# Block-sparse attention and an MLP: neighbouring values reloaded once a batch, neighbouring keys multiplied where they lie

## The chip, the cores and the metric

The kernel runs on one core of a Trainium2 chip. The metric is the device time of one execution in microseconds. A core has TensorE (PE in the profile, with its weight loads listed apart as PEld), VectorE (DVE), ScalarE (ACT), GpSimd (POOL) and SyncE (SP, which here issues DMAs only). Each engine takes its own queue in order, and semaphores hold it where its data is not ready.

## The reference

Block-sparse attention over q, k, v of (4 batches, 8 heads, 768 positions, 64), then an MLP over the 3072 tokens of 512 values:

```python
scores = np.matmul(q, k.transpose(0, 1, 3, 2)) / np.sqrt(D)
mask = np.abs(blk_i - blk_j) <= 1                      # blocks of 32, 24 of them
mask |= (blk_i == 0) | (blk_j == 0) | (blk_i == 23) | (blk_j == 23)
for qb in range(24):
    for kb in sampled_blocks[qb]:                      # 3 random blocks
        mask[qb*32:(qb+1)*32, kb*32:(kb+1)*32] = True
attn = softmax(np.where(mask, scores, -1e9))
x = np.matmul(attn, v).transpose(0, 2, 1, 3).reshape(3072, 512)
h = x @ w_in                                           # 512 x 2048
g = np.maximum(h, 0) ** 2
out = g @ w_out                                        # 2048 x 512
```

Inputs and output are float32; `sampled_blocks` (24, 3) is read at run time.

## The kernel before

All arithmetic on the chip has bf16 operands and float32 sums. Two heads share the 128 partitions, so there are 16 units u (batch u // 4, head pair u % 4). The stages are:

**Batches 0 and 1: dense.** Scores of 256 queries (places q0 = 0, 256, 512) against all keys (`scores`), `exps` on ACT, a product with 0/1 masks on DVE (`masks`), `values` with a column of ones for the sum, `normalize` on DVE (L387: a reciprocal at L391 and a product at L393 into a tile `xq` of one unit). In batch 1 each unit's `xq` is then transposed into the tile xT by a DMA that SP issues (`x_transp_dma`, L415); xT holds the four units of a place, and the MLP tile of that place waits for all four.

**Batches 2 and 3: sparse, in six visits v.** A visit takes two groups g = 2v and 2v+1 of 64 queries. Group 0 holds the first and last block, which see all keys (6 chunks of 128). Every other group sees 3 chunks: chunk 0 is the neighbouring four blocks, chunks 1 and 2 hold the two edge blocks and six sampled ones.
- Keys: `k_gather` (L548, on POOL or DVE) loads the sampled block numbers into registers (`blocks_of`, L531), then copies from the transposed keys QKT into the tile KG: chunk 0 (L558), the edge blocks where they are not there yet (L561, L562) and six sampled ones (L564).
- Values: `v_store` (L509) writes the batch's values VB to DRAM as rows. For each visit `v_gather` (L538) fetches the sampled rows into the tile VG (an indirect DMA on POOL, L543, or block by block from SP with register offsets, L546), and `v_window` (L516) the edge rows (L524) and the neighbouring rows (L528).
- `s_scores` (L566) multiplies, `s_exps` (L585, ACT), `s_masks` (L591, DVE), `s_values` (L597), `s_normalize` (L621, DVE, tile `xs`) and `s_transp` (L629, a DMA transpose into xT).

**The table** of the visits (`table_slots`, L452 on) is worked out once from the sampled blocks: row numbers for the indirect DMAs and the masks MKS.

**The MLP** runs in tiles of 256 tokens: `hidden` (four 128-wide slices of d_ff into one PSUM tile), `relu` (ACT L671 or DVE L673), `square`, `output`, `out_copy`, `store`. `w_load` brings the weights through POOL's queue.

Matrix products whose contraction fits use `pair` (L186): the same product on the two halves of 64 rows of the array, one after the other (form 64*128 in the profile). The sparse `s_values` at L618 uses 128 rows and 64 columns (128*64), the first batch's `values_full` and a few others 128*128.

The order of all work is written out: each step is a Task, and `PROGRAM` (L932) is a string of words, each an engine letter, a task number and, behind a slash, a PSUM spot. `run_program` goes through it and hands each instruction to its engine's queue in that order; `Buf` counts who holds a rotating buffer. So an engine is never rescheduled: an instruction that waits holds up all behind it on its engine. The raw inputs pass through `cast_qk` (float32 to bf16, L118 in the profile for all `copy` on POOL or DVE) and `transp_dma`.

The functions that are touched follow, with the profile's line numbers.

Of the kernel before, what the change touches and what calls it, by code (L numbers as in the profile page):

```python
# [19 lines left out]
P = 128  # L20
# [5 lines left out]
def kernel(  # L26
# [65 lines left out]
    def run_program(bufs):  # L92
# [3 lines left out]
        for word in PROGRAM.split():  # L96
            i, _, spot = word[1:].partition("/")
            t = tasks[int(i)]
            assert not t.done and all(d.done for d in t.deps)
            for b in t.get:  # L100
                if b.pool == "X":
                    b.at = int(spot)
                    old, cells[b.at] = cells[b.at], b
                else:
                    taken[b.pool].append(b)
# [21 lines left out]
    raw = {}  # L127

    def load(u, w, e):
        b, a = divmod(u, HP)  # L130
        name = ("qs", "ks", "vs")[w]
        t = ld.tile([P, 2, NCH, D], F32, name=name, tag=name, bufs=NRAW - (w > 0))
# [9 lines left out]
    KGT = [consts.tile([P, HP, 2, 3 * P], BF, name=f"KG{i}") for i in range(KG_BUFS)]  # L142

    def load_part(eng, u, w, ns):
        if u not in raw:
            raw[u] = [ld.tile([P, 2, NCH, D], F32, name=n, tag=n, bufs=NRAW - (n != "qs")) for n in ("qs", "ks", "vs")[:3 if u < 2 else 1 if u == 2 else 0]]
            if u == 2:
                raw[u] += [KGT[0].rearrange("p a i c -> p (a i c)").bitcast(F32)[:, 0:2 * NCH * D]]
            elif u == 3:
                raw[u] += [KGT[i].rearrange("p a i c -> p (a i c)").bitcast(F32)[:, j:j + 2 * NCH * D] for i, j in ((0, 2 * NCH * D), (1, 0))]  # L150
            if u >= 2:
                raw[u].append(work.tile([P, 2 * d_model], F32, name="ys", tag="ys", bufs=YS_BUFS))
# [25 lines left out]
    place = work.tile([P, TWM], F32, name="r", tag="r", bufs=R_BUFS).bitcast(BF)[:, 0:S]  # L178
# [39 lines left out]
    pre = work.tile([P, TWM], F32, name="r", tag="r", bufs=R_BUFS)[0:nb]  # L218
# [29 lines left out]
    MK, vg_at, vg_of = {}, {}, {}  # L248
    VGT = [consts.tile([P, 6 * H * VR], BF, name=f"VG{i}") for i in range(VG_BUFS)]

    def mk_claim(c0, e):
        MK[c0] = VGT[len(vg_at) % VG_BUFS][:, 0:NCH * QW].rearrange("p (n c) -> p n c", n=NCH)
        vg_at[c0] = len(vg_at) % VG_BUFS
# [19 lines left out]
    def cast_qk(u, w, ns, e):  # L273
        c = work.tile([P, NCH, 2, D], BF, name="qc", tag="qc", bufs=QC_BUFS)[:, ns]
# [68 lines left out]
    def exps(a, e):  # L343
        n = a[2] * len(a[3])
        pT = work.tile([P, 2, 512], BF, name="pT", tag="pT", bufs=PT_BUFS)
# [40 lines left out]

    def normalize(u, q0, w, e):  # L387
# [4 lines left out]
        xq = work.tile([P, 2, 2, D], BF, name="xq", tag="xq", bufs=XQ_BUFS)[:, 0:n]  # L392
        V.tensor_tensor(out=xq.rearrange("p c h d -> p h c d"), in0=po[:, :, :, 0:D], in1=rs.broadcast_to([P, 2, n, D]), op=AOP.mult)  # L393
        xtile[u, q0] = xq
# [11 lines left out]
    def x_tile(b, c0):  # L406
        if (b, c0) not in xT:
            xT[b, c0] = work.tile([P, HP, QW], BF, name="xT", tag="xT", bufs=XT_BUFS)
# [22 lines left out]
    dup, low = consts.tile([GR, SL - 4], F32, name="dup"), {}  # L431
    HB = block // 2
# [11 lines left out]
    def table_places(e):  # L444
        G.iota(ids[:, 0:4], pattern=[[1, 4]], base=0, channel_multiplier=2, **small)
# [6 lines left out]
    def table_slots(e):  # L452
        tmp = work.tile([P, TWM], F32, name="r", tag="r", bufs=R_BUFS)
# [4 lines left out]
        low[0] = work.tile([P, TWM], F32, name="r", tag="r", bufs=R_BUFS)[0:D].bitcast(BF)[:, 0:5 * P].rearrange("g (s c) -> g s c", c=P)  # L458
# [4 lines left out]
        for s_ in range(n):  # L463
            V.tensor_reduce(out=dup[:, s_:s_ + 1], in_=eq[:, s_, 0:4 + s_], axis=AX.X, op=AOP.max)
# [11 lines left out]
        def spread(j, of):  # L476
            to = low[0][0:GR, j].rearrange("g (k i) -> g k i", i=HB)
            V.tensor_copy(out=to[:, 0:RS], in_=of[:, 6:SL, None].broadcast_to([GR, RS, HB]))
            V.tensor_copy(out=to[:, RS:n], in_=of[:, 4:6, None].broadcast_to([GR, 2, HB]))

        for a in range(2):
            V.tensor_copy(out=low[0][0:GR, a].rearrange("g (e k i) -> g e k i", e=2, i=HB), in_=al[:, None, a, 0:4, None].broadcast_to([GR, 2, 4, HB]))
            spread(2 + a, al[:, a])
        spread(4, ids)
# [27 lines left out]
    def v_claim(b, v, e):  # L512
        vg_at[b, v] = len(vg_at) % VG_BUFS
        vgt[b, v] = VGT[vg_at[b, v]].rearrange("p (s c) -> p s c", s=6)
# [23 lines left out]
    def v_gather(b, v, i, e):  # L538
# [3 lines left out]
        if e == "POOL":  # L542
            G.indirect_dma_start(out=to[0:RS * HB], out_offset=None, in_=pairs, in_offset=bass.IndirectOffsetOnAxis(ap=idx[0:RS * HB, g - 1:g], axis=0))  # L543
        else:
            for j, r in enumerate(blocks_of(g, mybir.EngineType.SP)):
                sy.dma_start(out=to[j * HB:(j + 1) * HB], in_=pairs[bass.ds(r * HB, HB)])  # L546

    def k_gather(b, v, g, e):  # L548
# [7 lines left out]
        to = KGT[n][:, :, g % 2].bitcast(I32).rearrange("p a (z e j) -> p a z e j", z=3, e=2)  # L556
        rows = to[:, :, 1:3].rearrange("p a z e j -> p a z (e j)")
        eng.tensor_copy(out=to[:, :, 0], in_=src[:, :, :, 2 * w * (g - 1):2 * w * (g + 1)])  # L558
        if there.get((n, g % 2)) != b:
            there[n, g % 2] = b  # L560
            eng.tensor_copy(out=rows[:, :, :, RS * w:(RS + 1) * w], in_=src[:, :, :, 0:w])  # L561
            eng.tensor_copy(out=rows[:, :, :, (RS + 1) * w:], in_=src[:, :, :, (nb - 1) * w:nb * w])  # L562
        for r_ in range(RS):
            eng.tensor_copy(out=rows[:, :, :, r_ * w:(r_ + 1) * w], in_=src[:, :, :, bass.ds(at[r_] * w, w)])  # L564

    def s_scores(u, v, gs, buf, e):  # L566
        b, a = divmod(u, HP)
        i, ps, at = u % NPB, tile_of(buf), 0
        for g in gs:
            for c in range(chunks_of(g)):  # L570
                def keys(rows):
                    if g == 0:
                        return QK[i][rows, 1].rearrange("r (e p m) -> r e m p", e=2, m=CP)[:, c % 2, c // 2]
                    return KGT[kgt[b, v]][rows, a, g % 2, c * P:(c + 1) * P]
# [6 lines left out]
                pair(lambda h: ps[:, h, at:at + D], lambda h, rows: keys(rows), lambda h, rows: queries(rows), start=at == 0, stop=True)  # L581
# [3 lines left out]
    def s_exps(u, v, gs, e):  # L585
        n = sum(D * chunks_of(g) for g in gs)
        pT = work.tile([P, 2, 512], BF, name="pT", tag="pT", bufs=PT_BUFS)
# [33 lines left out]
    def s_normalize(b, v, e):  # L621
# [3 lines left out]
        xs = work.tile([P, HP, 2, D], BF, name="xs", tag="xs", bufs=2)  # L625
# [35 lines left out]
    def relu(T, f, e):  # L661
# [3 lines left out]
        r = work.tile([P, TWM], F32, name="r", tag="r", bufs=R_BUFS)[:, 0:n * w]  # L665
# [9 lines left out]
        gunit[T, f] = work.tile([P, TWM], BF, name="g", tag="g", bufs=G_BUFS)  # L675
# [45 lines left out]
    def out_copy(T, i, y, e):  # L721
        w = y[1] * (y[2][1] - y[2][0])
        ys = work.tile([P, 2 * d_model], F32, name="ys", tag="ys", bufs=YS_BUFS)[:, 0:w]
# [29 lines left out]

    def prepare(u):
# [4 lines left out]
        if u >= HP:  # L759
            g = gate[GATES[min(u - HP, len(GATES) - 1)]]  # L760
            old = [u - HP if u < HP + n_ else u - n_ for n_ in (NRAW, NRAW - 1, NRAW - 1)]
            ld_t = [T_(load, u, w, deps=cq[old[w], w] + [g]) for w in range(3)]
            at = [ld_t[2]]
            for w in (1, 0):
                qc = Buf("qc")
                c = T_(cast_qk, u, w, ALL, get=[qc], deps=[ld_t[w]])
# [3 lines left out]
        else:  # L770
            at = []
            for w, ns in [(1, ns) for ns in (KEYS if u == 0 else (ALL,))] + [(0, ns) for ns in QRS]:
                qc, hb = Buf("qc"), Buf("X")
                c = T_(cast_qk, u, w, ns, get=[qc])
# [4 lines left out]
        cv[u] = [T_(cast_v, u, deps=at + old_v)]  # L779
# [6 lines left out]

    def x_get(b, c0):
        if (b, c0) in xb:
            return {}
        xb[b, c0] = Buf("xT")  # L790
        return dict(get=[xb[b, c0]])

    def attend(a, add):
        u, q0, w, cs = a
        xb_, st, pt = Buf("X"), Buf("S"), Buf("pT")
        deps = [ev[u][1, n] for n in cs] + [ev[u][0, n] for n in range(q0 // P, (q0 + w) // P)]
# [222 lines left out]
```

## Time and profile before

| | us |
|---|---|
| runs | 266.87, 271.15, 262.80 |
| median of the 3 | 266.87 |
| the profiled execution | 263.07 |
| its span, first to last instruction | 261.3 |
| PE busy, 20 to 100 us of the span (first dense batches, MLP begins) | 79.05 of 80 |
| PE busy, 100 to 220 us (sparse batches, MLP) | 111.46 of 120 |
| PE busy, 220 to 261.3 us (last sparse visits, MLP) | 37.25 of 41.3 |

The mean granted clock of TensorE is 0.993. The costliest groups of the page, as far as the change touches them:

| line, operation | count | busy us | mean ns |
|---|---|---|---|
| L188 matmul of scores from KG, 64*128, 64 columns | 528 | 16.1 | 192 |
| L543 indirect DMA of sampled rows (POOL) | 21 | 20.1 | 958 |
| L564 copy of a sampled key block (POOL) | 114 | 25.0 | 265 |
| L558 copy of the neighbouring keys (POOL) | 19 | 8.1 | 428 |
| L118 cast of q (POOL) | 19 | 10.3 | 567 |
| L118 cast of k (POOL) | 13 | 8.8 | 699 |

How to read it: the span lies inside the time, which has 1.8 us around it. A matmul's own duration (192 ns) is from its start to the end of its flow through the array; matmuls overlap, so the pace is read from starts. "Busy" is the union of such times. What a line in square brackets or behind an arrow names is the event that ended an engine's idle time. Profile times are one execution's, while the runs differ by 3% among themselves.

### The profile page before, as it was taken

How to read it: one execution, taken by the hardware profiler on the slowest of the kernel's cores; microseconds unless marked ns; L12 is line 12 of the kernel's file. 1: busy time of each engine (PE TensorE's matmuls, PEld its weight loads, DVE VectorE, ACT ScalarE, POOL GpSimd, SP SyncE). 2: the span in 40 equal slices, each digit the busy share in tenths (PEclk: the TensorE clock that was granted, in tenths of full speed). 3: DMA queues.
4: the chain of work that ended last, by engine and by line, in shares of the span. 5: the costliest groups of instructions: out<-in, count | busy, mean ns of one | idle time of the engine just before them, and what ended most of it. 6: DMA issues, size and time to landing. Idle time of an engine off the chain costs nothing.

```text
span 261.3 us, 12047 instructions
## 1 busy us (share of the span) xinstructions
PE 244.1 (93%) x5265; PEld 186.4 (71%) x5265; DVE 155.5 (60%) x332; ACT 185.4 (71%) x218; POOL 118.1 (45%) x260
## 2 busy tenths in 40 slices
PE   6898999999999999986799989899999997999993
PEld 4766888679776599854676869757767775767683
DVE  7588879798989888574085634757646433520000
ACT  1799999999999899856397527855765857234640
POOL 2355571112046102496076797486475871143220
PEclk9999999999999999999799999999999999999999
DMA  6999999999879959959997999995953755112022
GB/s 183 373 266 176 251 180 272 215 239 238 222 243 205 220 136 208 171 130 231 228 241 160 204 203 224 245 236 107 264 118 116 160 95 151 23 23 80 3 99 67
DMA packets 64627, 47.08 MB, mean 180 GB/s; under 512 B 31599, under 2 KB 60656, under 8 KB 64576
## 3 DMA queue, kind: packets, MB, share of 16 engines
q1 hardware_dynamic: 58464, 37.48, 63.6%
q0 software_dynamic: 5568, 8.45, 18.3%
q8 instruction: 41, 0.67, 1.1%
q10 hardware_dynamic: 544, 0.39, 0.5%
q14 instruction: 10, 0.08, 0.1%
HBM read 35.51 MB, written 7.91 MB: 166 GB/s over the span
## 4 chain that ended last, share of the span: by engine, by line
PE 81%; DVE 6%; DMA 5%; ACT 4%; issue 2%; SPq 1%; DVEq 1%; POOL 0%; ACTq 0%; POOLq 0%
PE X L188 74%; PE X L618 4%; ACT pT L346 3%; DMA xT<-xq 2%; DMA xT<-xs 2%; PE X L384 2%; DVE pT L595 2%; DVE r L673 1%; SPq L417 1%; DVE QKT L118 1%; ACT pT L588 1%; DVE xq L393 0%; DVEq L533 0%; PE X L291 0%; DVE KG L564 0%
## 5 line engine op out<-in xcount | busy, mean ns | idle before, releaser
L188 PE MATMUL X<-xT,w_in_sb 64*128 64x256 bf16 x1536 | 101.9, 271 | 5.8 <-DMA xT<-xq 4.0
L188 PE MATMUL X<-w_out_sb,g 64*128 64x512 bf16 (+3 forms) x960 | 97.3, 334 | 1.4 <-issue 1.3
L188 PEld LDWEIGHTS <-w_in_sb 64*128 64x128 bf16 x1536 | 77.2, 95 | 18.0 <-issue 5.3
L346 ACT ACTIVATE pT<-X 128x1024 bf16<-128x1024 f32 x72 | 70.6, 1031 | 7.7 <-PE X L188 7.0
L588 ACT ACTIVATE pT<-X 128x768 bf16<-128x768 f32 (+1 forms) x56 | 41.5, 762 | 36.1 <-PE X L188 36.1
L188 PEld LDWEIGHTS <-g 64*128 64x128 bf16 x960 | 42.3, 94 | 25.2 <-issue 1.6
L684 POOL TENSOR_TENSOR g<-r 128x512 bf16<-128x512 f32 (+1 forms) x20 | 27.3, 1374 | 45.4 <-ACT r L671 27.2
L595 DVE TENSOR_TENSOR pT<-pT,MKS 128x768 bf16<-128x768 bf16 (+1 forms) x48 | 29.0, 637 | 23.1 <-ACT pT L588 23.1
L353 DVE TENSOR_TENSOR pT<-pT,VG 128x1024 bf16<-128x1024 bf16 x60 | 40.4, 708 | 2.1 <-ACT pT L346 1.9
L682 ACT ACTIVATE g<-r 128x1024 bf16<-128x1024 f32 (+1 forms) x40 | 37.2, 944 | 3.4 <-DVE r L673 3.2
L671 ACT ACTIVATE r<-X 128x1024 f32<-128x1024 f32 x27 | 28.5, 1064 | 14.0 <-PE X L188 13.6
L188 PE MATMUL X<-QKT 64*128 64x256 bf16 (+1 forms) x384 | 31.9, 254 | 1.0 <-DVE QKT L118 0.7
L673 DVE TENSOR_SCALAR r<-X 128x1024 f32<-128x1024 f32 x21 | 25.6, 1222 | 11.7 <-PE X L188 7.1
L564 POOL COPY KG<-QKT 128x64 int32 x114 | 25.0, 265 | 0.0
L543 POOL DMA_INDIRECT VG<-rows,idx x21 | 20.1, 958 | 10.2 <-DMA rows<-VB 3.7
L188 PEld LDWEIGHTS <-QKT 64*128 64x128 bf16 x384 | 16.5, 97 | 5.8 <-issue 1.0
L118 POOL CAST qc<-qs 128x384 bf16<-128x384 f32 (+3 forms) x19 | 10.3, 567 | 20.3 <-DMA qs<-in_q_dram 17.5
L188 PEld LDWEIGHTS <-KG 64*128 64x128 bf16 x528 | 14.6, 96 | 6.0 <-POOL KG L564 1.3
L118 POOL CAST qc<-ks 128x384 bf16<-128x384 f32 (+1 forms) x13 | 8.8, 699 | 21.3 <-DMA ks<-in_k_dram 18.9
L188 PEld LDWEIGHTS <-pT 64*128 64x128 bf16 x768 | 15.8, 94 | 3.1
L188 PE MATMUL X<-QKT,KG 64*128 64x64 bf16 x528 | 16.1, 192 | 1.5 <-POOL KG L564 0.8
L188 PE MATMUL X<-VB,pT 64*128 64x65 bf16 x768 | 17.4, 190 | 0.0
(101 smaller groups left out, 195.1 us busy)
## 6 DMA issues: line engine op xcount, KB each, us to landing
vs<-in_v_dram SPq DMA_DIRECT2D x14, 384.0 KB, 3.9
ks<-in_k_dram SPq DMA_DIRECT2D x13, 384.0 KB, 4.9
qs<-in_q_dram SPq DMA_DIRECT2D x12, 384.0 KB, 5.3
out_dram<-ys SPq DMA_DIRECT2D x9, 512.0 KB
VG<-rows SPq DMA_DIRECT2D x20, 132.0 KB, 6.6
w_in_sb<-in_moe_w_in_dram POOLq DMA_DIRECT2D x4, 512.0 KB, 9.0
w_out_sb<-in_moe_w_out_dram POOLq DMA_DIRECT2D x4, 512.0 KB, 7.6
rows<-VB SPq DMA_DIRECT2D x2, 792.0 KB
```

The source lines that it names most:

```text
L118: (V if e == "DVE" else G).tensor_copy(out=out, in_=in_)
L188: last = nc.tensor.matmul(out(r ^ crossed), lhsT(r ^ crossed, rows), rhs(r ^ crossed, rows), skip_group_check=True, **kw)
L346: A.activation(out=pT[:, :, 0:n], in_=stile.pop(a)[:, :, 0:n], func=AF.Exp, scale=scale)
L353: V.tensor_tensor(out=pT, in0=pT, in1=m[:, None].broadcast_to([P, 2, len(cs), w]), op=AOP.mult)
L543: G.indirect_dma_start(out=to[0:RS * HB], out_offset=None, in_=pairs, in_offset=bass.IndirectOffsetOnAxis(ap=idx[0:RS * HB, g - 1:g], axis=0))
L564: eng.tensor_copy(out=rows[:, :, :, r_ * w:(r_ + 1) * w], in_=src[:, :, :, bass.ds(at[r_] * w, w)])
L588: A.activation(out=pT[:, :, 0:n], in_=stile.pop((u, v, gs))[:, :, 0:n], func=AF.Exp, scale=scale)
L595: V.tensor_tensor(out=pT, in0=pT, in1=m[:, None].broadcast_to([P, 2, n]), op=AOP.mult)
L671: A.activation(out=to, in_=src, func=AF.Relu)
L673: V.tensor_scalar(out=to, in0=src, scalar1=0.0, scalar2=None, op0=AOP.max)
L682: A.activation(out=g, in_=r, func=AF.Square)
L684: (G if e == "POOL" else V).tensor_mul(out=g, in0=r, in1=r)
```

## The change

Six things, all in one edit:

1. Rotating buffers (raw inputs, r, ys, pT, g, qc, xq, xT) become named tiles; a Buf learns in `run_program` which of them it has, in the order of the plan.
2. In batch 1 the normalized values of the four units of a place go into one tile XS, and one `x_transp_dma` per place issues two transposes of 512 columns in place of four units' transposes of 256: 12 DMAs become 6.
3. Values: VB becomes the first six columns of a tile W of 11. After `v_store`, three `v_window` tasks a batch (two DMAs each) reload all 11 neighbouring windows into it, for all visits; the per-visit windows and the edge rows' DMAs are gone (24 and 12 DMAs before, 12 in all after). Visit 0 waits for all three windows, later visits for theirs. The gathers of sampled rows fetch the edge rows too (128 rows for 96); VG shrinks from six slots to four.
4. Keys: chunk 0 is no longer copied into KG (22 copies of 128x256 int32 are gone). It is multiplied where it lies in QKT, even and odd positions apart, as two pairs of 64 rows by 64 columns, each into half of the output partitions. The six chunks of group 0 are done in the same way. 272 matmuls of the form 64*128 become 544 of the form 64*64.
5. The table: eight reductions become one masked product and one reduction, six spreading copies become three, with one more iota.
6. A new PROGRAM. Of the 22 k_gathers, 13 are on POOL and 9 on DVE (19 and 3 before). Of the 22 v_gathers, three are on SP (one before). Of the q and k casts of units 4 to 15, 9 are on POOL and 15 on DVE (17 and 7 before). Three output copies move from ACT to DVE, and three of the table's mask casts too; three x copies of batch 0 likewise.

```diff
+    KGT = [consts.tile([P, HP, 2, 2 * P], BF, name=f"KG{i}") for i in range(KG_BUFS)]
+    W = [consts.tile([P, GR, H, VR], BF, name=f"W{i}") for i in range(2)]
...
-        VB.append(consts.tile([P, NCH, H, VR], BF, name=f"VB{i}"))
+        VB.append(W[i][:, 0:NCH])
...
-        xq = work.tile([P, 2, 2, D], BF, name="xq", tag="xq", bufs=XQ_BUFS)[:, 0:n]
+        b, a = divmod(u, HP)
+        xq = XS[:, :, a] if b else XQ[buf_of["xq", u, q0].at][:, 0:n]
...
-    def x_transp_dma(u, q0, w, e):
-        b, a = divmod(u, HP)
-        sy.dma_start(out=x_tile(b, q0)[:, a].rearrange("r (c p) -> r c p", p=P),
-                     in_=xtile.pop((u, q0)).rearrange("p c h d -> p (c h d)"), transpose=True)
-        otile.pop((u, q0))
+    def x_transp_dma(b, q0, e):
+        for c in range(2):
+            sy.dma_start(out=x_tile(b, q0)[:, :, c * P:(c + 1) * P], in_=XS[:, c].rearrange("p a h d -> p (a h d)"), transpose=True)
...
-        for s_ in range(n):
-            V.tensor_reduce(out=dup[:, s_:s_ + 1], in_=eq[:, s_, 0:4 + s_], axis=AX.X, op=AOP.max)
+        V.scalar_tensor_tensor(out=eq, in0=before, scalar=0.0, in1=eq, op0=AOP.is_gt, op1=AOP.mult)
+        V.tensor_reduce(out=dup, in_=eq, axis=AX.X, op=AOP.max)
...
-    def v_window(b, v, e):
-        gs = [g for g in VISITS[v] if g]
-        i0 = 2 - len(gs)
+    def v_window(b, w0, w1, e):
         w = H * VR
-        if vg_of.get(vg_at[b, v]) != b:
-            vg_of[vg_at[b, v]] = b
-            for j, r in enumerate((0, nb - 1)):
-                rows = rows_of[b][block * r:block * r + 1]
-                sy.dma_start(out=vgt[b, v][(RS + j) * HB:(RS + j + 1) * HB, 0:4],
-                             in_=bass.AP(rows.tensor, rows.offset, [[2 * w, HB], [0, 2], [1, 2 * w]]))
-        rows = rows_of[b][D * (gs[0] - 1):D * (gs[0] - 1) + 1]
+        rows = rows_of[b][D * w0:D * w0 + 1]
         for e_ in range(2):
-            sy.dma_start(out=vgt[b, v][e_ * D:(e_ + 1) * D, 4 + i0:6],
-                         in_=bass.AP(rows.tensor, rows.offset + e_ * w, [[2 * w, D], [D * w, 2 - i0], [1, w]]))
+            sy.dma_start(out=W[b % 2][e_ * D:(e_ + 1) * D, w0:w1].rearrange("p n h c -> p n (h c)"),
+                         in_=bass.AP(rows.tensor, rows.offset + e_ * w, [[2 * w, D], [D * w, w1 - w0], [1, w]]))
...
-            for j, r in enumerate(blocks_of(g, mybir.EngineType.SP)):
-                sy.dma_start(out=to[j * HB:(j + 1) * HB], in_=pairs[bass.ds(r * HB, HB)])
+            for j, r in enumerate([0, nb - 1] + list(blocks_of(g, mybir.EngineType.SP))):
+                sy.dma_start(out=to[j * HB:(j + 1) * HB], in_=pairs[r * HB:(r + 1) * HB] if j < 2 else pairs[bass.ds(r * HB, HB)])
...
     def k_gather(b, v, g, e):
...
-        eng.tensor_copy(out=to[:, :, 0], in_=src[:, :, :, 2 * w * (g - 1):2 * w * (g + 1)])
...
     def s_scores(u, v, gs, buf, e):
...
-                def keys(rows):
-                    if g == 0:
-                        return QK[i][rows, 1].rearrange("r (e p m) -> r e m p", e=2, m=CP)[:, c % 2, c // 2]
-                    return KGT[kgt[b, v]][rows, a, g % 2, c * P:(c + 1) * P]
+                def keys(rows, e):
+                    return QK[i][rows, 1].rearrange("r (e j) -> r e j", e=2)[:, e, D * c:D * (c + 1)] if g == 0 else QK[i][rows, 1].rearrange("r (e j) -> r e j", e=2)[:, e, block * (g - 1):block * (g + 1)]
...
-                pair(lambda h: ps[:, h, at:at + D], lambda h, rows: keys(rows), lambda h, rows: queries(rows), start=at == 0, stop=True)
+                if g and c:
+                    pair(lambda h: ps[:, h, at:at + D], lambda h, rows: KGT[kgt[b, v]][rows, a, g % 2, (c - 1) * P:c * P], lambda h, rows: queries(rows),
+                         start=at == 0, stop=True)
+                else:
+                    for e_ in range(2):
+                        pair(lambda h: ps[e_ * D:(e_ + 1) * D, h, at:at + D], lambda h, rows: keys(rows, e_), lambda h, rows: queries(rows),
+                             start=at == 0, stop=True)
                 at += D
...
-                        if g == 0:
-                            val = VB[b % 2][:, c].rearrange("p h c -> p (h c)")[:, cols]
-                        elif c == 0:
-                            val = vgt[b, v][:, 4 + i, cols]
+                        if c == 0 or g == 0:
+                            val = W[b % 2].rearrange("p n h c -> p n (h c)")[:, g - 1 if g else 2 * c, cols]
...
-        parts.append(T_(v_window, b, v, deps=[vw, cl]))
+        parts += [wins[i] for i in ((0, 1, 2) if v == 0 else sorted({(g - 1) // 4 for g in VISITS[v]}))]
...
+            wins = [T_(v_window, b, w0, min(w0 + 4, GR), deps=[vw]) for w0 in range(0, GR, 4)]
```

More of the change, by code (lines that the diff above doesn't have):

```diff
@@ L177 @@
     V.memset(bm, 0.0)
-    place = work.tile([P, TWM], F32, name="r", tag="r", bufs=R_BUFS).bitcast(BF)[:, 0:S]
+    place = RT[0].bitcast(BF)[:, 0:S]
     blk = consts.tile([P, nb + 1], F32, name="blk")
@@ L217 @@
     edge = consts.tile([nb, 2], F32, name="edge")
-    pre = work.tile([P, TWM], F32, name="r", tag="r", bufs=R_BUFS)[0:nb]
+    pre = RT[1][0:nb]
     pm = pre[:, 0:2 * nb].rearrange("q (i j) -> q i j", i=2)
@@ L273, in cast_qk @@
     def cast_qk(u, w, ns, e):
-        c = work.tile([P, NCH, 2, D], BF, name="qc", tag="qc", bufs=QC_BUFS)[:, ns]
+        c = QC[buf_of["qc", u, w, ns.start].at][:, ns]
         if w < 2 and u >= SB * HP:
@@ L344, in exps @@
         n = a[2] * len(a[3])
-        pT = work.tile([P, 2, 512], BF, name="pT", tag="pT", bufs=PT_BUFS)
+        pT = PT[buf_of["pT", a].at]
         A.activation(out=pT[:, :, 0:n], in_=stile.pop(a)[:, :, 0:n], func=AF.Exp, scale=scale)
@@ L407, in x_tile @@
         if (b, c0) not in xT:
-            xT[b, c0] = work.tile([P, HP, QW], BF, name="xT", tag="xT", bufs=XT_BUFS)
+            xT[b, c0] = XTT[xb[b, c0].at]
         return xT[b, c0]
@@ L444, in table_places @@
     def table_places(e):
+        G.iota(before, pattern=[[1, SL - 4], [-1, SL]], base=4, channel_multiplier=0, **small)
         G.iota(ids[:, 0:4], pattern=[[1, 4]], base=0, channel_multiplier=2, **small)
@@ L452, in table_slots @@
     def table_slots(e):
-        tmp = work.tile([P, TWM], F32, name="r", tag="r", bufs=R_BUFS)
+        tmp = RT[tb["tmp"][0].at]
         n = SL - 4
@@ L664, in relu @@
         n, w = per_unit(T), T[2]
-        r = work.tile([P, TWM], F32, name="r", tag="r", bufs=R_BUFS)[:, 0:n * w]
+        r = RT[buf_of["r", T, f].at][:, 0:n * w]
         to = r.rearrange("p (h c) -> p h c", h=2)
@@ L674, in relu @@
         rltile[T, f] = r
-        gunit[T, f] = work.tile([P, TWM], BF, name="g", tag="g", bufs=G_BUFS)
+        gunit[T, f] = GT[buf_of["g", T, f].at]
     def square(T, f, i, n, e):
@@ L760, in prepare @@
             g = gate[GATES[min(u - HP, len(GATES) - 1)]]
-            old = [u - HP if u < HP + n_ else u - n_ for n_ in (NRAW, NRAW - 1, NRAW - 1)]
-            ld_t = [T_(load, u, w, deps=cq[old[w], w] + [g]) for w in range(3)]
+            for w in range(3):
+                raw_of[u, w] = Buf(RAWS[w])
+            ld_t = [T_(load, u, w, get=[raw_of[u, w]], deps=[g] + raw_claims[-1:]) for w in range(3)]
             at = [ld_t[2]]
@@ L771, in prepare @@
             at = []
+            own = range(3 if u < 2 else 1 if u == 2 else 0)
+            for w in own:
+                raw_of[u, w] = Buf(RAWS[w])
+            if own:
+                raw_claims.append(T_(raw_claim, u, get=[raw_of[u, w] for w in own], deps=raw_claims[-1:]))
             for w, ns in [(1, ns) for ns in (KEYS if u == 0 else (ALL,))] + [(0, ns) for ns in QRS]:
                 qc, hb = Buf("qc"), Buf("X")
-                c = T_(cast_qk, u, w, ns, get=[qc])
+                c = T_(cast_qk, u, w, ns, get=[qc], put=[raw_of[u, w]] if (u, w) in raw_of else [])
+                buf_of["qc", u, w, ns.start] = qc
                 cq.setdefault((u, w), []).append(c)
```

231 lines of the change are left out of this document (128 added, 103 removed).

## The prediction

> **What bounds the kernel now.** I began with the busy shares at the head of the page and the shares of the chain that ended last.
>
> ```profile
> PE 244.1 (93%) x5265; PEld 186.4 (71%) x5265; DVE 155.5 (60%) x332; ACT 185.4 (71%) x218; POOL 118.1 (45%) x260
> ```
>
> ```profile
> PE 81%; DVE 6%; DMA 5%; ACT 4%; issue 2%; SPq 1%; DVEq 1%; POOL 0%; ACTq 0%; POOLq 0%
> ```
>
> TensorE is busy 93% of the span and is 81% of the chain, so whatever lengthens its queue lengthens the kernel. The change acts on batches 2 and 3, so I then cut the stage in which they run into windows (columns: window, its length, busy time of PE, PEld, DVE, ACT and POOL with instructions, granted clock, DMA share, GB/s).
>
> ```profile
> 100.00:120.00 20.00, 19.23 (x426) 15.05 (x422) 13.12 (x28) 16.04 (x21) 12.96 (x36) 1.00 0.97 184
> 120.00:140.00 20.00, 15.85 (x363) 12.53 (x358) 9.90 (x19) 12.74 (x16) 9.61 (x25) 0.91 1.03 203
> 140.00:160.00 20.00, 18.60 (x383) 14.65 (x381) 7.91 (x18) 9.85 (x12) 14.19 (x34) 1.00 1.15 207
> 160.00:180.00 20.00, 19.30 (x416) 14.72 (x414) 13.63 (x18) 12.99 (x18) 15.01 (x44) 1.00 1.02 216
> 180.00:200.00 20.00, 20.00 (x496) 14.32 (x494) 11.50 (x24) 13.85 (x17) 10.21 (x21) 1.00 0.60 147
> 200.00:220.00 20.00, 18.48 (x380) 13.67 (x372) 8.99 (x15) 14.44 (x16) 13.93 (x34) 1.00 0.61 146
> ```
>
> PE idles 0.77 + 4.15 + 1.40 + 0.70 + 0 + 1.52 = 8.5 us in 120; no other engine is above 80%. Queue order and transfers can win back at most those 8.5 us and what the low clock of 120 to 140 cost; anything else has to come from, or go to, the matmuls.
>
> So I read PE's timeline (start, time to the last end, tile form, count). A new group starts when its first matmul starts, so the starts are the clock.
>
> ```profile
> 113.70 1.89 PE L188 MATMUL X<-w_out_sb,g 64*128 64x512 bf16 x16
> 115.42 0.34 PE L188 MATMUL X<-QKT,KG 64*128 64x64 bf16 x12
> 115.60 1.03 PE L188 MATMUL X<-w_out_sb,g 64*128 64x512 bf16 x8
> ```
>
> ```profile
> 142.32 1.89 PE L188 MATMUL X<-w_out_sb,g 64*128 64x512 bf16 x16
> 144.14 0.95 PE L618 MATMUL X<-VG,pT 128*64 128x65 bf16 x48
> 145.02 0.61 PE L188 MATMUL X<-xT,w_in_sb 64*128 64x256 bf16 x8
> ```
>
> Twelve score matmuls take 115.42 to 115.60, 15 ns each, two row halves overlapping. L618's 48 take 0.88 us, 18.3 ns each. The same sixteen w_out matmuls take 1.72 us ahead of another 64*128 group and 1.82 us ahead of the 128*64 one: 0.1 us for the change of tile form. I measured all 38 places of the trace where successive matmuls differ in form (24 between 64*128 and 128*64, 14 between 64*128 and 128*128): the next start comes 123 to 126 ns after a 65-column matmul where 31 to 33 per pair is the pace, 199 to 202 after 256 columns (pace 105), 305 after 512 (pace 213). That is 93 ns each time. The weight loads tell the same:
>
> ```profile
> 144.14 0.84 PEld L618 LDWEIGHTS <-pT 128*64 128x64 bf16 x48 [0.42 <-issue]
> ```
>
> ```profile
> 115.21 0.43 PEld L188 LDWEIGHTS <-KG 64*128 64x128 bf16 x12
> ```
>
> Inside one form the first weights go in 0.21 us before their matmul (115.21 against 115.42); at the change they start with it, at 144.14, after an idle 0.42 us. The load is not hidden there, because the array is emptied first.
>
> **The change, part by part.**
>
> *Tile forms on PE.* A neighbouring chunk was one pair of 64*128 matmuls from a copy; now it is two pairs of 64*64, and so is every chunk of group 0. 272 matmuls become 544. In the built order chunk 0 stands before chunks 1 and 2 for each group, so a two-group score task changes form four times and the 16 tasks of visit 0 twice: 40×4 + 16×2 = 192, less 8 fewer changes elsewhere: 222 against 38, or +184. The trace has no change between 64*128 and 64*64. By the nearest rows, 93 ns for all 38 changes of the three forms it has, it costs 184 × 0.093 = 17.1 us; the other end is 0, if only a change of the row split (64 against 128 rows) empties the array. Every change of the trace is one of that kind too, so it cannot tell; I take 93 ns, because the price was the same for two different pairs of forms, one with a column split and one without. Nothing hides it: PE's queue is in order and nearly full.
>
> The Trainium skill, "TensorEngine Tiling (Array Packing)", Key Properties, says that changing the tiling mode, not just the tile, drains TensorE, and its list of configurations has 64×64 and 64×128 as different modes; that speaks against this change. The trace agrees for the three modes it holds; 64×64 no run here shows yet.
>
> The 272 extra matmuls cost 272 × 15 ns = 4.1 us at the pace of the 12-matmul row. Ends: 0 if four quadrants overlap as two halves do, and 544 × 18.3 − 272 × 15 = 5.9 us at L618's pace. I take 4.1, the row of the same operands.
>
> The Trainium skill, "TensorE: Matmul & The Clock Gate", Back-to-back issue gap, gives about 25 ns as the least gap of a small matmul; an estimate by it is 272 × 25 = 6.8 us, and the sum below would be 280.3. The 15 ns of the row are less than that floor, so the row decides.
>
> *Stalls that go.* The largest idle of the stage is this:
>
> ```profile
> 125.77 0.82 PE L188 MATMUL X<-xT,w_in_sb 64*128 64x256 bf16 x6 [4.04 <-DMA xT<-xq]
> ```
>
> The chain shows its cause in order: a DVE k_gather (`L533`, register load 1.23 us at 111.48, copies to 114.5) between the two last normalizes of batch 1, then SP transposes of 1.2 us each, then the last transpose, 5.95 us from issue to landing (1.24 issue, 4.7 flight). After it the clock is 0.5 for 3.41 us and w_in pairs take 213 instead of 109 ns: 1.65 us lost. In the new order both normalizes stand ahead of the k_gathers, two wide transposes replace the four narrow ones, and PE has 5 scores' worth more of other work: 8 s_scores, 7 output, 4 hidden and 1 s_values between the place's last values and the first w_in of its tile, about 10.3 us against 6.7. Needed are 0.6 + 2 × 1.2 + 4.7 = 7.7 us, or 10.3 if the four window issues (0.65 us each) that stand ahead on SP all fall in between. So I let it go, 4.04 + 1.65. The same for 1.52 us at 218.99 (a transpose behind an SP v_gather of 207.64 to 211.66), 0.77 for POOL's KG at 112.35 (POOL loses 19 first-chunk copies, 8.1 us) and 0.70 for DVE's r. Together 8.7 us; with slower PE these gaps close anyway. Ends: 10 (all idle here and the clock) and 4.0 (the last normalizes still late).
>
> *New waits.* Nine k_gathers now sit on DVE instead of three, each a register load of 1.2 to 1.65 us and six copies of 0.19, about 25 us in place of 8; r, masks and normalizes queue behind them. The stage has 55 us of idle DVE and PE is slower there, so they are covered; without that cover each hits its masks and then s_values by up to 2.8 us. SP has three v_gathers instead of one (1.86 us register load, eight issues of 0.5), and visit 0 waits for six window DMAs at 0.65 us; s_values of batch 3's first visit has about 10 us of PE work after the last window issue. Against that SP loses 30 small issues. I put 2.0 us, ends 0 and 8 (three late masks).
>
> *Edits at nothing.* Names of tiles: no instruction. Table: 8 reduces become 2 operations, hidden in the first 100 us, where nothing waits for it. Gathers of 128 instead of 96 rows: same bytes as the edge DMAs they replace. Copies moved between ACT, DVE and POOL: below each engine's idle, bar one case, the third rival below.
>
> *The sum.* 263.07 + 17.1 + 4.1 − 8.7 + 2.0 = 277.6 us on the profiled execution (span 261.3 and 1.8 around it). The median of the runs is 266.87, 3.8 higher; on it the sum is 281.4. I predict 279, between the two. Own range: 270 (263.07 + 17.1 − 10, all cheap ends but the change of form) to 294 (all dear ends, on the median).
>
> **The rivals.**
> *No emptying between 64*128 and 64*64* because the row split stays: 263.07 + 4.1 − 8.7 + 2.0 = 260.5, 1% faster, within what can be told. For it: no row here has this change. Against it: the even price of all 38 changes.
> *The four quadrants run side by side with no emptying, and the stalls go.* Then 544 matmuls cost what 272 did, and the order decides: 263.07 − 8.7 = 254.4, 3.3% faster. It decides if the 64*64 starts come below 8 ns apart and the sum of new waits is under 3.4 us. For it: two row halves overlap so today (15 ns for 64 columns). Against: 64*128 and 128*64 cost a full 93 ns though both have two tiles. The skill's page on tiling, Key Properties, says tiles load and multiply in parallel, which the 15 ns bear out for two.
> *Casts on DVE.* POOL waited 18.9 and 17.5 us for loads, harmlessly:
>
> ```profile
> POOL qc L118 <- DMA ks<-in_k_dram: 18.9, 2, 13.0
> POOL qc L118 <- DMA qs<-in_q_dram: 17.5, 4, 6.5
> ```
>
> Eight of its 17 later casts move to DVE, which has only 10.6 us idle between 20 and 100 us. The share 36.4 × 8/17 = 17 us exceeds that by 6.5, with masks and normalizes waiting behind: 277.6 + 6.5 = 284.
> That the change does not do what it says is ruled out by the built order, which has the 64*64 matmuls and none of the 22 first-chunk copies.
>
> **How the numbers follow.** Forecast 0.69, DVE casts 0.08, no emptying 0.13, quadrants 0.10. By 2%, about what a measurement of this kernel can tell (its three runs spread 3%): the first two are slower (0.77), the third the same (0.13), the fourth faster (0.10). The range runs from 263 (no emptying, counted on the median: 264) to 290 (263.07 + 17.1 + 5.9 − 4 + 8), leaving out the quadrants and the very dear end.
>
> **What would show it.** Right: starts at each change between 64*64 and 64*128 about 120 ns apart, their weight loads starting with the matmul after "issue", PE near 20 of 20 in every window from 105 to 240, that stage some 15 us longer, and the 4.04 us before xT gone with the clock at 1.00. Wrong: starts of 30 ns at those places (first or second rival); PE idle in 20 to 100 us with DVE casts as releaser (third); or an idle of several us before the first s_values of a batch, on the window loads.

## The result and the profile after

| | before | changed |
|---|---|---|
| median of 6 runs each, us | 266.85 | 284.88 |
| range, us | 262.80 to 271.15 | 282.36 to 288.05 |
| ratio to before, 95% interval | | 1.078 (1.069 to 1.088) |
| span of the profiled execution, us | 261.3 | 284.5 |
| PE busy in it, us | 244.1 | 266.7 |

The ratio, like those of the experiments, is of the fast runs alone, without those over 1.5% above the fastest of their kernel; by the medians of all six it is 1.068. The changed kernel is 18 us slower by the medians. The spans of the profiled executions say where: they differ by 23.2 us (the one execution, 263.07 us, lies 4 us under its kernel's median, the other, 286.85, 2 us over), and 22.6 of that is more PE busy time; PE's idle went from 17.2 (261.3 − 244.1) to 17.8 us. So the matmuls grew, and the stalls were not won back. The page's first part and the head of its fourth, for the changed kernel:

```profile
PE 266.7 (94%) x5537; PEld 191.2 (67%) x5537; DVE 166.7 (59%) x376; ACT 183.1 (64%) x215; POOL 92.0 (32%) x187
```

```profile
PE 82%; ACT 5%; DVE 4%; DMA 4%; issue 3%; SPq 1%; another core or an unknown queue 0%; DVEq 0%
```

Every engine but PE and DVE has less to do, POOL by over a fifth (118.1 to 92.0 us), and none of it counts, since PE's share of the chain is still above 80%. The windows (columns as before) show the two halves of the story:

```profile
20.00:100.00 80.00, 76.25 (x1649) 59.24 (x1651) 70.02 (x148) 72.89 (x82) 19.85 (x33) 1.00 1.01 220
100.00:120.00 20.00, 16.56 (x450) 13.77 (x446) 12.63 (x28) 15.47 (x17) 5.92 (x14) 1.00 1.31 210
120.00:140.00 20.00, 17.69 (x356) 11.09 (x356) 8.83 (x34) 9.79 (x14) 5.35 (x18) 0.91 0.83 165
140.00:160.00 20.00, 19.90 (x402) 12.46 (x396) 11.52 (x30) 11.01 (x13) 11.06 (x19) 1.00 0.74 146
160.00:180.00 20.00, 18.90 (x344) 13.18 (x346) 11.51 (x28) 11.52 (x14) 5.05 (x8) 1.00 0.78 188
180.00:200.00 20.00, 19.91 (x482) 13.45 (x476) 7.29 (x14) 10.76 (x14) 12.83 (x37) 1.00 0.84 180
200.00:220.00 20.00, 20.00 (x398) 13.18 (x396) 7.39 (x21) 13.32 (x17) 10.40 (x23) 1.00 0.32 88
```

From 140 us on PE's longest idle is 0.72 us (at 170.35; from 220 to 260 us it is busy for 39.99 of 40), the other engines and the DMA (shares of at most 0.84) have room, and yet PE gets through no more matmuls than before: 1626 from 140 to 220 us, where it was 1675. From 20 to 140 us, where the kernel before lost 0.95 + 0.77 + 4.15, the new one loses 3.75 + 3.44 + 2.31, and the clock dips to 0.91 in the same window of 120 to 140 as it did. PE's timeline of one score task shows what fills the late windows (start, time to the last end, form, count):

```profile
152.07 0.22 PE L200 MATMUL X<-QKT 64*64 64x64 bf16 x4
152.23 0.23 PE L200 MATMUL X<-QKT,KG 64*128 64x64 bf16 x4
152.39 0.22 PE L200 MATMUL X<-QKT 64*64 64x64 bf16 x4
152.55 0.23 PE L200 MATMUL X<-QKT,KG 64*128 64x64 bf16 x4
152.61 0.60 PE L200 MATMUL X<-xT,w_in_sb 64*128 64x256 bf16 x8
```

A group of four matmuls starts every 0.16 us, where twelve took 0.18 us in the kernel before. The task takes 152.07 to 152.61, 0.54 us, for the work of those twelve. The weight loads of the same stretch:

```profile
152.07 0.11 PEld L200 LDWEIGHTS <-QKT 64*64 64x64 bf16 x4 [0.21 <-issue]
152.22 0.12 PEld L200 LDWEIGHTS <-KG 64*128 64x128 bf16 x4
152.39 0.11 PEld L200 LDWEIGHTS <-QKT 64*64 64x64 bf16 x4
152.54 0.11 PEld L200 LDWEIGHTS <-KG 64*128 64x128 bf16 x4
```

Each group's loads start within 0.01 us of its matmuls instead of ahead of them: the same sign as at L618 before. At 217 of the trace's 222 changes of form the weight load starts 1 to 5 ns ahead of its matmul; inside one form the median is 45 ns.

Over the whole trace there are 88 blocks of four 64*64 matmuls. By the medians a block's first start is 120 ns behind the last 64*128 start, its own starts are 3.3 ns apart, and the next 64*128 start comes 146 ns behind its last: 276 ns. In the kernel before, the pair of 64*128 matmuls in its place takes three intervals of 26, 3 and 26 ns, 55 in all. So a block costs 221 ns more and a change of form (276 − 55) / 2 = 110 ns. The extra matmuls cost next to nothing: four take 10 ns from first to last start, where the pair takes 3. The four quadrants do run side by side. (The expectations below count 16 ns for each interval of before, and so 235 ns a block.)

The longest waits of the changed kernel that PE itself paid for (us in total, times, longest):

```profile
PE X L200 <- issue: 4.5, 4, 2.3
PE X L200 <- DMA QKT<-qc: 1.8, 1, 1.8
PE X L200 <- DMA xT<-XS: 1.4, 1, 1.4
```

The transposes into xT cost 1.4 us in place of 4.0, and those of the sparse visits none. But "issue", PE waiting for nothing that the profile names, went from 1.3 to 4.5 us, and a transpose of q and k is late by 1.8 us.

### The profile page after: what moved, and what is told of

It is laid out like the page before. It is cut to its first block, busy times and chain, and to the rows that moved or that the text cites. A ratio compares the mean times of both kernels' runs of the same rounds, so it can differ in the third digit from the quotient of the medians.

```text
span 284.5 us, 12546 instructions
## 1 busy us (share of the span) xinstructions
PE 266.7 (94%) x5537; PEld 191.2 (67%) x5537; DVE 166.7 (59%) x376; ACT 183.1 (64%) x215; POOL 92.0 (32%) x187
## 4 chain that ended last, share of the span: by engine, by line
PE 82%; ACT 5%; DVE 4%; DMA 4%; issue 3%; SPq 1%; another core or an unknown queue 0%; DVEq 0%
PE X L200 75%; PE X L625 4%; ACT pT L357 3%; DMA QKT<-qc 2%; PE X L395 2%; DMA xT<-XS 2%; ACT g L690 1%; DVE r L681 1%; DVE pT L364 1%; PE X L302 1%; DVE QKT L119 1%; DVE VG L276 0%; SPq L437 0%; DVE W L119 0%; DVE xq L410 0%
## 5 line engine op out<-in xcount | busy, mean ns | idle before, releaser
L200 PEld LDWEIGHTS <-w_in_sb 64*128 64x128 bf16 x1536 | 74.6, 94 | 18.2 <-issue 3.6
L200 PEld LDWEIGHTS <-g 64*128 64x128 bf16 x960 | 40.4, 94 | 27.1 <-issue 0.6
L200 PE MATMUL X<-QKT 64*64 64x64 bf16 (+1 forms) x832 | 52.8, 232 | 5.7 <-issue 2.3
L200 PEld LDWEIGHTS <-QKT 64*64 64x64 bf16 (+1 forms) x832 | 27.2, 102 | 25.9 <-issue 16.9
L604 DVE TENSOR_TENSOR pT<-pT,MKS 128x768 bf16<-128x768 bf16 (+1 forms) x48 | 24.1, 534 | 23.2 <-ACT pT L597 22.8
L200 PE MATMUL X<-QKT,KG 64*128 64x64 bf16 x352 | 20.4, 195 | 0.0
L569 POOL COPY KG<-QKT 128x64 int32 x78 | 15.5, 245 | 13.5 <-PE X L200 13.4
L200 PE MATMUL X<-W,pT 64*128 64x65 bf16 x768 | 17.3, 190 | 1.0 <-issue 0.9
L631 DVE RECIPROCAL ss<-X 128x8 f32<-128x8 f32 x12 | 2.5, 205 | 21.8 <-PE X L625 16.6
L625 PEld LDWEIGHTS <-pT 128*64 128x64 bf16 x624 | 11.6, 111 | 2.1 <-issue 1.9
```

Of the source, the lines that this page charges most:

```text
L200: last = nc.tensor.matmul(out(r ^ crossed), lhsT(r ^ crossed, rows), rhs(r ^ crossed, rows), skip_group_check=True, **kw)
L569: eng.tensor_copy(out=rows[:, :, :, (2 + r_) * w:(3 + r_) * w], in_=src[:, :, :, bass.ds(at[r_] * w, w)])
L604: V.tensor_tensor(out=pT, in0=pT, in1=m[:, None].broadcast_to([P, 2, n]), op=AOP.mult)
L625: nc.tensor.matmul(po[i * D:(i + 1) * D, h, a * VW:(a + 1) * VW], pts[g][:, h, c * D:(c + 1) * D], val, start=a == 0 and c == 0, stop=c == ...
```

## The experiments

Theory A: the changes of form are the loss. Theory B: the new order and its waits are the loss, and the longer matmuls only fill time that PE would have waited. Theory C: the price goes by the number of matmuls and weight loads.

### Copied keys (e1)

```diff
-KGT = [consts.tile([P, HP, 2, 2 * P], BF, ...
+KGT = [consts.tile([P, HP, 2, 3 * P], BF, ...
+eng.tensor_copy(out=to[:, :, 0], in_=src[:, :, :, 2 * w * (g - 1):2 * w * (g + 1)])
...
-if g and c:
-    pair(..., KGT[kgt[b, v]][rows, a, g % 2, (c - 1) * P:c * P], ...)
+if g:
+    pair(..., KGT[kgt[b, v]][rows, a, g % 2, c * P:(c + 1) * P], ...)
```

> The changed kernel with the 22 first-chunk copies back in KG and groups above 0 multiplied in the form 64*128 again; group 0 stays 64*64. To make room the g tiles go from 12 to 10. In the changed kernel's trace a block of four 64*64 matmuls takes 120 ns from the last 64*128 start, 3 x 5.5 inside and 146 ns to the next 64*128 start, 283 ns, where three intervals of 16 ns stood before: 235 ns more, times 88 blocks = 20.7 us. Theory A (the changes of form are the loss): 284.9 - 20.7 = 264.2, up to 269 if the shorter PE queue uncovers waits. Theory B (the new order and its waits are the loss, and the matmuls only fill time in which PE would have waited): 278 or more.

Measured: 263.21 us (258.23 to 264.61) beside 261.86 us (260.51 to 264.78) for the kernel before on the same chip. Theory A expected 264.2, theory B 278. PE busy falls by 21.4 us with the changes of form, which go from 222 to 50:

```profile
PE 245.3 (94%) x5361; PEld 182.7 (70%) x5361; DVE 169.3 (65%) x385; ACT 182.1 (70%) x215; POOL 97.4 (37%) x200
```

One view of the same score work, PE's timeline of this kernel:

```profile
143.19 0.34 PE L200 MATMUL X<-QKT,KG 64*128 64x64 bf16 x12
143.37 0.60 PE L200 MATMUL X<-xT,w_in_sb 64*128 64x256 bf16 x8
```

Twelve matmuls in 0.18 us again. Theory B falls. Everything else in the change is still in this kernel, except that two of the twelve g tiles made room for the copies, and by the medians it ends 0.5% from the kernel before: the rest is worth nothing that can be told.

### Grouped (e2)

```diff
-for g in gs:
-    for c in range(chunks_of(g)):
+steps = [(g, c, (j * 3 + c) * D) for j, g in enumerate(gs) for c in range(chunks_of(g))]
+for g, c, at in sorted(steps, key=lambda s: s[0] > 0 and s[1] > 0):
```

> The changed kernel with the neighbouring chunks of both groups of a score task multiplied first and then the gathered chunks: the same matmuls, two changes of form per task in place of four in 40 tasks. Theory A: 40 x 0.24 = 9.6 us less, 275.3. Theory B, or a loss that goes by the number of matmuls: 283 to 286.

Measured: 274.14 us, ratio 1.036 (1.026 to 1.046) to the kernel before, against 1.078 for the changed kernel. The difference of 0.042 is 11 us. By the medians the two kernels are 10.7 us apart too, but the kernel before was 5 us faster beside e2 than beside the changed kernel (261.86 and 266.85); what decides is PE busy, which falls by 11.1 us. Theory A expected 275.3, the others 283 to 286. No matmul was added or taken away (5537 in both); 80 changes of form were. PE's timeline of one task:

```profile
145.78 0.26 PE L200 MATMUL X<-QKT 64*64 64x64 bf16 x8
145.96 0.29 PE L200 MATMUL X<-QKT,KG 64*128 64x64 bf16 x8
146.09 0.60 PE L200 MATMUL X<-xT,w_in_sb 64*128 64x256 bf16 x8
```

0.31 us for the task instead of 0.54. This is the cleanest of the tests for A, since only the order of the same matmuls inside a task differs.

### The kernel before with one chunk, and with all, in 64*64 (e3, e4)

```diff
-pair(lambda h: ps[:, h, at:at + D], lambda h, rows: keys(rows), ...)
+if g and c == 0:          # e4: if g
+    for e_ in range(2):
+        pair(lambda h: ps[e_ * D:(e_ + 1) * D, h, at:at + D], lambda h, rows: keys(rows)[:, e_ * D:(e_ + 1) * D], ...)
+else:
+    pair(lambda h: ps[:, h, at:at + D], lambda h, rows: keys(rows), ...)
```

> The kernel before, where only the neighbouring chunk, still copied into KG, is multiplied as two pairs of 64*64: 176 more matmuls, 176 more changes of form, nothing else moved. Theory A: 88 x 0.235 = 20.7 us more, less what falls into the 8.5 us of idle of that stage: 279 to 288. Theory B: under 272.

> The kernel before, where all three chunks of the groups above 0 are multiplied as pairs of 64*64: 528 more matmuls, but only two changes of form per task, 96 in all. Theory A: 40 tasks of two groups at 120 + 23 x 5.5 + 146 - 13 x 16 = 184 ns and 8 of one group at 214 ns: 9.1 us more, 270 to 276. Theory C (the price goes by the matmuls and weight loads, 20.7 us for 176): 266.9 + 62 = 329.

Measured: e3 276.18 us, ratio 1.058 (1.053 to 1.064); e4 272.28 us, 1.042 (1.037 to 1.047). Three times as many extra matmuls cost less, so theory C falls (it gave 329 for e4). e3's 14.3 us over the kernel before on its chip lie inside theory A's 12 to 21 (its 279 to 288 started from 266.9, where this chip has 261.86): PE busy is 17.3 us more, and 4 us of PE's idle were filled. e4's 10.4 us are 1.3 above what was worked out.

The four kernels side by side, by PE busy in the profiled execution and by changes of form counted in the matmul records:

| pair of kernels | changes of form | PE busy, us | ns a change |
|---|---|---|---|
| changed → copied keys | 222 → 50 | 266.7 → 245.3 | 124 |
| changed → grouped | 222 → 142 | 266.7 → 255.6 | 139 |
| before → first chunk 64*64 | 38 → 209 | 244.1 → 261.4 | 101 |
| before → all chunks 64*64 | 38 → 121 | 244.1 → 254.7 | 128 |

### Casts on POOL (e6, e8, e10) and a second run of copied keys (e9)

The seven casts of q and k of units 4 to 11 that the new order gives to DVE go back to POOL, by their letters in PROGRAM alone, in the kernel with copied keys (e6, e10) and in the changed kernel (e8):

```diff
-... V256 ... V258 ... V272 ... V274 ... V282 ... V465 ... V457 ...
+... G256 ... G258 ... G272 ... G274 ... G282 ... G465 ... G457 ...
```

> The kernel with copied first chunks and the seven casts of q and k of units 4 to 11 that the changed order has on DVE given back to POOL. Theory F (DVE casts hold up the dense stage): PE's idle of 20 to 100 us goes from 3.2 us to 1.5 or less, and the time falls by 1.7 to 2.5 us against the kernel with copied chunks. Else (POOL's waits for loads hold up its k_gathers, or the idle has another cause): no fall, or 1 to 3 us more.

> The changed kernel, forms of its matmuls as they are, with the seven casts of q and k of units 4 to 11 back on POOL. If the loss in the dense stage and the loss by the forms add up: PE's idle of 20 to 100 us goes from 3.75 to about 1.8 us and the time falls by about 2 us, ratio to the kernel before near 1.07. If the shorter dense stage only meets the same waits later: ratio as the changed kernel's, 1.078.

> The kernel with copied first chunks once more, on the chip of the run beside it, so that the two differ in the forms and the seven casts alone. Forms alone are worth 21.4 us of PE busy time (266.7 against 245.3); with 2 us for the casts this kernel should be 17 to 21 us under the other, and within 1% of the kernel before.

> The kernel with copied first chunks and casts on POOL a second time, on another chip. It was 0.986 of the kernel before (0.976 to 0.996), while the kernel with copied chunks alone was 1.014 on its second chip. If the casts are worth what they did in the changed kernel (1.078 to 1.066), it should come out at 1.00, not at 0.986; if it is faster than before for good, below 0.993.

Measured, ratios to the kernel before on each one's own chip: e8 1.066 (1.060 to 1.071) against the changed kernel's 1.078; e9 1.014 (1.010 to 1.019); e6 0.986 (0.976 to 0.996); e10, the same kernel as e6, 1.019 (1.012 to 1.027). The window of the dense stage in the kernel with copied keys, and then in e6:

```profile
20.00:100.00 80.00, 76.77 (x1700) 60.10 (x1697) 70.10 (x149) 74.20 (x83) 21.78 (x35) 1.00 1.07 226
```

```profile
20.00:100.00 80.00, 77.72 (x1715) 61.49 (x1713) 69.53 (x146) 75.86 (x84) 28.44 (x42) 1.00 1.10 230
```

The same window in e8, beside 76.25 in the changed kernel:

```profile
20.00:100.00 80.00, 77.77 (x1711) 60.85 (x1707) 68.94 (x146) 75.26 (x84) 28.60 (x42) 1.00 1.12 228
```

PE's idle there goes from 3.23 to 2.28 us in e6 (1.5 or less was expected), from 3.75 to 2.23 in e8 (about 1.8 expected), and from 3.43 in e9 to 2.33 in e10. In all three pairs the wait for QKT at 63 to 65 us (1.6 to 1.9 us) is gone, and in all three the wait for XS that ends at 99 to 103 us is longer: 1.26 us in place of 0.26, 1.63 in place of 1.45, 1.24 in place of 0.41. So the casts on DVE did hold up the dense stage, by some 2 us ahead of that wait, of which up to 1 is lost again in it. What that is worth in time is not shown: e8's ratio is 0.012 under the changed kernel's, but the two were not measured side by side, and e6 and e10 are one kernel, whose ratios differ by 3% with intervals that do not touch. Differences of 2% between kernels on different chips are not to be read here. e10's 1.019 is neither the 1.00 nor the 0.993 that its expectation names, and e9's 1.014 is just outside the 1% that was expected. No kernel of this study is faster than the kernel before in a way that came back.

e8 and e9 ran side by side on one chip: 279.46 and 264.19 us, 15.3 apart. They differ in the forms (PE busy 264.9 and 245.4 us), in two g tiles and, the other way, in the casts (about 2 us of idle), so 17 to 21 was expected, and it fell a little short.

### The transposes first (e7)

```diff
-... S537 S602 P419 P898 S495 S601 V420 V499 P489/3 S421 ... V433 G500 ... S408 ...
+... S537 P419 P898 S495 V420 P489/3 S421 ... V433 V499 G500 ... S408 S602 S601 ...
```

V499 is the DVE k_gather, V420 and V433 the last normalizes, S421 and S408 transposes into xT, S602 and S601 raw loads.

> The kernel before, where SP issues the three last transposes of batch 1 ahead of two raw loads (0.59 and 1.22 us) and DVE makes its k_gather behind both last normalizes; nothing else moved. If SP's queue set the 4.04 us of PE idle, the transposes land 1.8 us earlier and about 2.2 us of idle are left, with or without the half clock behind it: 2 to 3.5 us less than before, ratio 0.987 to 0.993. If DVE's k_gather set it, the idle goes below 1.2 us and the time falls by 3 to 5 us. If the stall only moves to the next wait: no change.

Measured: 263.44 us (257.25 to 271.32) beside 263.67 (259.93 to 268.85), ratio 0.986 (0.974 to 0.998), no clear difference by what e6 and e10 showed, as the last of the three outcomes has it. The stall of 4.04 us is gone from its place. A wait of 1.70 us for DVE's r stands at 118.45 us, and this has come 1.4 us later in the span than the old stall:

```profile
127.14 1.05 PE L188 MATMUL X<-xT,w_in_sb 64*128 64x256 bf16 x16 [3.42 <-DVE xs L626]
```

The chain of the kernel says how (start, length, what):

```profile
119.46 5.68 DMA ks<-in_k_dram
...
125.70 0.54 DVE qc L118
126.25 0.13 DVE ss L624
...
126.40 0.70 DVE xs L626
```

The raw load of k that was moved back is issued at 119.46 us, where the kernel before issued it at 115.95; DVE's cast waits for it, and the next normalize stands behind the cast. SP issues one transfer right behind the other from 97.9 to 129.9 us here, so what gives way in its queue is late itself.

### Fewer window loads (e5)

```diff
-for e_ in range(2):
+for e_ in range(2 if b > SB or w0 == 0 else 0):
...
-[:, g - 1 if g else 2 * c, cols]
+[:, (g - 1 if g else 2 * c) % (GR if b > SB else 4), cols]
```

> The kernel with copied first chunks, without the reloads of windows 4 to 10 of batch 2 (four DMAs); batch 2 reads windows 0 to 3 in their place, so its values are left wrong. In the kernel with copied chunks PE idles 0.98, 0.65 and 1.86 us on 'issue' up to 106.98, 112.56 and 118.53 us, each 1.4 to 1.6 us behind the landing of a 16 KB packet of the instruction queue. Theory D (instruction packets come late because the DMA engines are crowded, share 1.2 to 1.4 there): the three together under 1 us. Theory E (PE runs through its instructions faster than they are fetched, whatever the other transfers): they stay near 3.5 us.

Measured: 263.98 us, ratio 1.006 (0.995 to 1.016). The three idles are 0.86, none and 0.75, together 1.6 us, between the two theories. And in e9, which has all its window loads, they are 0.85, none and 0.32. So the idles vary that much between executions of one kernel, and e5 does not tell what makes them long or short.

## Why the prediction was right

The time, the sign and the main mechanism came out as forecast: 279 predicted, 284.88 measured, in the range of 263 to 290. One term of the sum did not. On the profiled execution, for which it was written, the sum of 277.6 is 9.3 us short of 286.85: 7.3 by the stalls and waits (−6.7 forecast, +0.6 measured), 1.4 by the matmuls (21.2 against 22.6 us of PE busy time) and 0.6 by the time around the span (1.8 and 2.4 us). That 279 lies nearer to the median is in part luck, since the two profiled executions lie on opposite sides of their medians. Of the signs of being right, the starts and weight loads at the changes came, and PE near 20 of 20 came from 140 us on instead of 105; the clock of 1.00 from 120 to 140 did not come. By its steps:

**Changes of form: right, a little low.** The first step extended 93 ns a change, seen only between other forms, to 64*64. It is 110 ns at the blocks, 101 to 139 by the four pairs of kernels above. On the way into a block the 93 ns hold (120 ns where 26 is the pace); on the way out of a block of four it is 120 (146 against 26). For 184 changes 17.1 us were put down; 184 × 0.110 is 20.2. The rule of the Trainium skill, "TensorEngine Tiling (Array Packing)", Key Properties, that a changed tiling mode drains TensorE, is borne out for 64×64 against 64×128 by e2, where the order alone of the same matmuls gave back 11.1 us of PE busy time.

**Extra matmuls: too dear.** 4.1 us were put down, at 15 ns each. The starts inside a block are 3.3 ns apart, and a block of four takes 10 ns against 3 for the pair that it replaces: 0.6 us for 88 blocks. The lower end, 0, was nearly the true one. With the step above, 21.2 us were forecast for the two and 21.4 came back when the keys were copied again: two errors of 3 to 4 us that cancel, which is luck.

**Stalls that go: the step that failed.** "Together 8.7 us" were to be won and 2.0 given back, −6.7. Measured are +0.6 us of PE idle. Of the 8.7, the idle before xT fell from 4.04 to 1.45 us and the 1.52 and 0.77 us went; the 0.70 us for DVE's r stayed (0.72 at 170.35); the half clock stayed, for 3.41 us as before, at a new idle of 2.31 us. What was won came back as waits that the sum does not have: "issue" went from 1.3 to 4.5 us, and in the dense stage there are 1.8 us for QKT and 1.3 for a cast. From 100 to 240 us the idle is 7.05 us where it was 8.54 from 100 to 220, and 20 to 100 us lost 2.8 more. The chain of the kernel before led me to blame DVE's k_gather; e7 moved it, together with two loads, and the last transpose was issued 2.2 us earlier (SP's four end at 118.8 us in place of 121.0), but only by making another transfer of SP's full queue late. That slower matmuls close gaps "anyway" was right only from 140 us on, where 1.3 of 120 us are idle; the new gaps lie earlier, in the dense stage and up to 122.80 us, while the first 64*64 matmul starts at 112.57.

**New waits: misplaced.** The 2.0 us were for DVE and SP in the sparse stage. A price of that size was paid in the dense stage, by the casts, as the third rival has it; it came to some 2 us, not 6.5, and beside the price of the forms, not in its place. The 3.2 us more of "issue" stand in neither.

**The rivals.** The first (no emptying) gave 260.5; e2 rules it out. The second was half right: the quadrants do run side by side, and the emptying eats it all. The third is the one just told. The cover of the copies was seen correctly: 22 copies of the neighbouring keys put back in e1 cost PE nothing that shows.

**What stays open** is why PE's instructions came late. That 4.3 of the 4.5 us of "issue" are PE waiting for them is shown at the end; what makes these idles long or short from one execution to the next was not found.

## What to carry to other kernels

Before a small copy is traded for more and smaller matmuls, count the places where successive matmuls differ in their rows and columns, in the order in which they will be issued, and price each as the trace prices such a place; here 184 of them cost some 20 us, and the copies that they saved were hidden. If two forms are needed, put all matmuls of one form together first: that halved the price here without any other edit. And a stall that hangs on a full queue is not won by moving its last entry: list what else stands in that queue, since it is late next.

## What was not expected of the hardware

- On the way into a block of 64*64 matmuls a change of form costs the same whatever stands ahead: the next start comes 120 ns behind 64-column matmuls, 199 behind 256 columns and 306 behind 512, where 26, 106 and 213 are the pace without a change, so 93 or 94 ns more. On the way out it costs less when the block is longer: the next start comes 146 ns behind blocks of four, 125 ns behind blocks of 8, 12 or 24 (e2, e4).
- Inside a block of four, the starts are 3.3 ns apart. In blocks of 24 it is 8.2 ns on average: four starts 3 or 4 ns apart and then, as a rule, 21 or 22 ns to the next four.
- PE's idles of "issue" are waits for its own instructions. The instruction queue brings packets of 16 KB: 43 in the changed kernel, whose PE has 11074 matmuls and weight loads, 41 for 10530 in the kernel before, 45 for 11586 in e4, some 257 to a packet each time. The changed kernel's three long idles of this kind, up to 110.41, 116.27 and 122.80 us, begin when PE has started 4281, 4536 and 4790 of them, so one packet apart. The traces of e1, e6, e8 and e10 have idles at the same three counts, those of e2, e5 and e9 at two of the three. And each ends behind the landing of a packet (108.96, 114.83, 121.25), by 1.45, 1.44 and 1.55 us. Of the 42 such idles over 0.15 us in the twelve traces 41 end 1.2 to 1.9 us behind a landing, and one 2.7. PE's timeline of the changed kernel at the three:

```profile
110.41 2.23 PE L200 MATMUL X<-xT,w_in_sb 64*128 64x256 bf16 x37 [1.07 <-issue]
116.27 0.38 PE L200 MATMUL X<-W,pT 64*128 64x65 bf16 x13 [0.92 <-issue]
122.80 0.42 PE L200 MATMUL X<-QKT 64*64 64x64 bf16 x14 [2.31 <-issue]
```

The last of these stands inside a block of 64*64 matmuls. The transfer of the packet began when PE had some 50, 95 and 30 instructions left, counted at 255 to a packet; from 200 us on packets begin to come with 118 to 286 left. The late ones lie in a stretch with a DMA share of 1.31, the others where it is 0.2 to 0.3. Whether that crowding is the cause is not shown: the length of such idles differed between executions of one kernel with the same transfers (0.98, 0.65, 1.86 in e1 and 0.85, none, 0.32 in e9).
